# A two-layer product in float32 halves, whose first token block takes its second layer from undivided float32 operands

## The chip, the core and the metric

The kernel runs on one core of one Trainium2 chip. The metric is the device time of one execution in microseconds. Five engines with queues of their own work side by side: TensorE (PE, with its weight loads shown as PEld), VectorE (DVE), ScalarE (ACT), GpSimd (POOL) and SyncE (SP), which here issues most transfers. Each executes its queue in order, and an instruction that waits holds up all that stands behind it.

## The reference, cut to what matters

```python
def _moe_ref(x, w_in, w_out):          # x 4608 x 512, w_in 512 x 2048, w_out 2048 x 512
    h = x @ w_in
    g = h - np.tanh(h)
    return (g @ w_out).astype(np.float32)

def reference(**kwargs):
    attn_out = _attn_ref(q, k, v)      # softmax over q and over k, then two small products
    x = attn_out ... reshape(4608, 512)
    x = _moe_ref(x, w_in, w_out)
    return _moe2_ref(x, ...)           # each token to one of 8 experts, two layers, scaled
```

The weights w_in and w_out come as 64-bit floating point numbers. The change touches only the product g @ w_out of the first 512 tokens, and what has to be moved because of it.

## The kernel before, in words

The 4608 tokens are worked in NB = 9 blocks of 512. Within a block, the inner size 2048 goes in NCH = 16 chunks of 128. One chunk of one block is a slot s, from 0 to 143, with block j = s // 16 and chunk c = s % 16. The program is written out slot by slot: at(slot, order, function) files a step, and run_slot issues the steps of a slot in the order of their second number. That is the order of every engine's queue.

A float32 product is made of three products of a faster type, F32R. Each operand a is divided into a high part (ScalarE copies it into F32R) and a low part (the rest, subtracted on VectorE or GpSimd), and high x high, high x low and low x high are added up. Per slot the steps are:

- l1(s), at 0.30: the first layer, hps = w_in[c] x, 12 matmuls of 128 x 512 (4 parts of the depth, 3 products each).
- gfn(s), at 0.50: ScalarE makes gt and gy from hps, VectorE makes gg from them in two instructions (lines 246, one reading hps from the accumulator memory, one reading gy and gg).
- gsplit(s), at 0.90: gg is divided into gh (ScalarE, L687) and gl (L691). In block 0, gl is on GpSimd for three of four slots, and on VectorE otherwise.
- l2(s - 2), at 0.70: the second layer, four token tiles of 128, each with 3 matmuls of 128 x 512 (L706) into acc0 to acc3.

In block 0 the weights are still being made ready. Each slot loads two pieces of the 64-bit weights (load_pair, into raw and rawb), VectorE decodes them into float32 with integer operations (decode1 at 0.85: two of L243, four of L246, written to ta), ScalarE copies the high parts and GpSimd subtracts for the low parts (decode2 at 0.60, L298 and L300: woh and wol for w_out, wih and wil for w_in). From block 1 on all weights stay in memory.

Beside this, a KUnit per two heads prepares the next block's attention: a maximum over tokens (mx, tp, top, bc), subtraction, exponential, a product pk. For blocks 0 and 1 the maximum over partitions is made by a transposition on TensorE (pm, L374), a reduction on VectorE (mm, L378) and a matmul (L381). For blocks from 2 on it is one GpSimd instruction (red, L389). The unit of block j + 1 runs in block j, so the unit of block 2 runs in block 1. xmm makes the next block's x (px, L633, then xth on ScalarE and xtl on VectorE, L638 and L639); two of its four parts stand at the end of slot 15, two at the start of slot 16. The tiles pm, pk, pt and px take turns in two buffers of one tag "m" of the accumulator memory.

In block 1 a Router for block 0's output is added: rows of dot products on VectorE (rjk, L754), and at slot 30 four indirect transfers issued from GpSimd (L851).

Of the kernel before, what the change touches and what calls it, by code (L numbers as in the profile page):

```python
# [10 lines left out]
F32 = mybir.dt.float32  # L11
F32R = mybir.dt.float32r
# [60 lines left out]
def moe_kernel(ctx, tc, q, q_t, k_t, v_t, w_in, w_out, emb, tau, w1, w2, out, dbg=None):  # L73
# [108 lines left out]
    def full_run(general):  # L182
# [16 lines left out]

        wop.tile([P, 96], F32, name="pad1")  # L200
        win_h, win_l, wout_h, wout_l = {}, {}, {}, {}
        raws = {}
        npair = [0]

# [16 lines left out]
        def wtiles(c, which):  # L221
            if which == 0:
                pool = wap if c < NWA else lazy["wb"]
            else:
                pool = wop
            nm = "io"[which]
            wh = pool.tile([P, KD, P], F32R, name=f"w{nm}h{c}")
            wl = pool.tile([P, KD, P], F32R, name=f"w{nm}l{c}")
            if which == 0:
                win_h[c], win_l[c] = wh, wl  # L230
            else:
                wout_h[c] = wh.rearrange("p k f -> p (k f)")
                wout_l[c] = wl.rearrange("p k f -> p (k f)")
            return wh, wl
# [18 lines left out]
        def decode1(keys):  # L253

            ch = staged[keys[0]] = []
            for i, key in enumerate(keys):
                raw = raws.pop(key)
                ch.append((raw[:, :, :, 0], raw[:, :, :, 1], itile(f"ta{i}")) + wtiles(*key))
            if general:
                return  # L260
            for lo, hi, ta, wh, wl in ch:
                ts(ta, hi, 0x07FFFFFF, AND, 3, LS)
            for lo, hi, ta, wh, wl in ch:
                stt(ta, hi, -0x40000000, ta, AND, OR)
            for lo, hi, ta, wh, wl in ch:
                stt(ta, lo, 29, ta, RS, OR)
# [9 lines left out]
        def bound(i):  # L276
# [12 lines left out]
            if i < len(guarded):  # L289
                t = lazy["sb"].tile([P, GW // 2, 2], I32, name="gw", tag="gw", bufs=OPT["gwb"])  # L290
                (nc.sync if OPT['gsp'] else nc.scalar).dma_start(out=t.rearrange("p f two -> p (f two)"), in_=guarded[i])
                gtiles[i] = t

        def decode2(keys, eng=nc.gpsimd):
            ch = staged.pop(keys[0])
            if not general:
                for lo, hi, ta, wh, wl in ch:
                    act(out=wh, in_=ta.bitcast(F32), func=AF.Copy)  # L298
                for lo, hi, ta, wh, wl in ch:
                    eng.tensor_tensor(  # L300
                        out=wl, in0=ta.bitcast(F32), in1=wh.bitcast(F32), op=ALU.subtract
                    )
                return
            for lo, hi, ta, wh, wl in ch:
                tb, tx = itile("tb"), itile("tx")
                ts(ta, hi, 0x7FFFFFFF, AND, 9, RS)
                ts(tb, hi, -0x80000000, AND)
                ts(ta, ta, float(-(896 << 11)), ALU.add, 0.0, ALU.max)
                ts(tx, hi, 0x1FF, AND)
                stt(ta, ta, 12, tb, LS, OR)  # L310
                act(out=wh, in_=ta.bitcast(F32), func=AF.Copy)
                stt(tx.bitcast(F32), lo.bitcast(U32), 2.0 ** -32, tx, ALU.mult, ALU.add)
                ts(tb, ta, -0x800000, AND)
                stt(wl, tx.bitcast(F32), 2.0 ** -20, tb.bitcast(F32), ALU.mult, ALU.mult)
# [18 lines left out]
        class KUnit:  # L333
# [101 lines left out]
            def schedule(self, s):  # L435
                if s:
                    at(s - 2, 0.65, self.load)
                    at(s - 2, 0.66, self.loadv)
                    late = self.b < 2
                    at(s if late else s - 1, 0.20 if late else 0.80, self.mx)  # L440
                if self.b < 2:
                    at(s, 0.75, self.tp)
                    at(s + 1, 0.19, self.top)
                    at(s + 1, 0.45, self.bc)
                else:
                    at(s, 0.01, self.red)
                at(s + 1, OPT['ks'] if self.b > 1 else OPT['ks1'], self.sub)
                at(s + 1, 0.85, self.exp)
                at(s + 2, OPT['kv'], self.kv)
                at(s + 2, 0.80, self.rs)  # L450
                at(s + 3, 0.20, self.out)
# [208 lines left out]
        def gfn(s):  # L660
            h = hps.pop(s)
            t = gp.tile([P, BT], F32, name="gt", tag="gt", bufs=2)
            y = gp.tile([P, BT], F32, name="gy", tag="gy")
            g = gp.tile([P, BT], F32, name="gg", tag="gg")
            act(out=t, in_=h, func=AF.Square)  # L665
            if not general:
                act(out=y, in_=t, func=AF.Square, bias=cqa[:, 0:1])
                stt(g, h, Q2, t, ALU.mult, ALU.mult)
                stt(g, y, QB, g, ALU.add, ALU.mult)
            else:  # L670
                th = gp.tile([P, BT], F32, name="gth", tag="gth")
                mk = gp.tile([P, BT], F32, name="gm", tag="gm")
                act(out=y, in_=t, func=AF.Square, bias=cpa[:, 0:1])
                act(out=th, in_=h, func=AF.Tanh)
                act(out=mk, in_=t, func=AF.Relu, bias=cnt2[:, 0:1])
                stt(g, h, C3, t, ALU.mult, ALU.mult)
                stt(y, y, PB, t, ALU.add, ALU.mult)
                dve.tensor_tensor(out=th, in0=h, in1=th, op=ALU.subtract)
                stt(g, y, PD, g, ALU.add, ALU.mult)
                dve.copy_predicated(g, mk.bitcast(I32), th)  # L680
            g_t[s] = (g, t)

        def gsplit(s):
            g, t = g_t.pop(s)
            gh = gp.tile([P, BT], F32R, name="gh", tag="gh", bufs=2 if general else 3)
            gl = gp.tile([P, BT], F32R, name="gl", tag="gl", bufs=2 if general else 3)
            act(out=gh, in_=g, func=AF.Copy)  # L687
            if not general:
                act(out=t, in_=t, func=AF.Square, accum_out=guard[:, s : s + 1])
            e = nc.gpsimd if s < NCH and s % OPT['gm'][0] < OPT['gm'][1] and not general else dve  # L690
            e.tensor_tensor(out=gl, in0=g, in1=gh.bitcast(F32), op=ALU.subtract)  # L691
            g_t[s] = (gh, gl)

        acc = {}
# [1 line left out]
        def l2(s):  # L696
            j, c = divmod(s, NCH)
            gh, gl = g_t.pop(s)
            for t in range(TPB):
                if c == 0:  # L700
                    acc[j, t] = ps_acc.tile([P, DM], F32, name=f"acc{t}", tag=f"acc{t}")
                sl = slice(t * P, (t + 1) * P)
                for i, (a, r) in enumerate(
                    ((gh, wout_h[c]), (gh, wout_l[c]), (gl, wout_h[c]))
                ):
                    pe.matmul(  # L706
                        acc[j, t], lhsT=a[:, sl], rhs=r,
                        start=(c == 0 and i == 0), stop=(c == NCH - 1 and i == 2),
                    )
# [565 lines left out]
        for c, ks in enumerate(pairs):  # L1275
# [2 lines left out]
                at(c - 2, OPT['d1'], decode1, ks)  # L1278
            at(c - 1, OPT['d2'], decode2, ks)

        for s in range(NS + 2):
            j, c = divmod(s, NCH)
            if s < NS:
# [306 lines left out]
```

## Time and profile before

| | us |
|---|---|
| median of 3 runs | 1361.91 |
| runs | 1361.67, 1361.91, 1365.99 |
| profiled execution, its own time | 1364.51 |
| its span in the trace | 1362.8 |

| engine | busy us | share of the span |
|---|---|---|
| PE | 1303.3 | 96% |
| DVE | 1067.4 | 78% |
| ACT | 782.5 | 57% |
| POOL | 348.5 | 26% |

The span is one profiled execution; the time around it is 1.7 us. Shares are averages over stages that differ: block 0 lies from about 28 to 152 us in the span, block 1 from there to about 250 us. In the timelines, "idle before" names what the engine waited for. Matmuls overlap their neighbours in the records, so the cost of one in a row of many is read from the distance between starts, not from its own length.

### The profile page before, as it was taken

Reading aid. Unit: us, or ns where it says so; the run is one execution under the profiler, and the core shown is the slowest. Engines: PE = TensorE matmul, PEld = TensorE weight load, DVE = VectorE, ACT = ScalarE, POOL = GpSimd, SP = SyncE. Lnnn points to the kernel's source line nnn. Section 1 sums busy time; section 2 is a strip of 40 time slices with the busy share of each in tenths; the row PEclk is TensorE's granted clock in tenths of the full one; section 3 lists DMA queues with packets and bytes.
Section 4 is the critical chain, followed back from the end, with each engine's and each line's share of the span. In section 5 each row is a group of like instructions: output and inputs, shape, how many; then the busy total and the mean of one; then the engine's idle time right before and its main releaser. Section 6 shows DMA issues by size and latency. Waiting matters only on the chain. (4 is left out here: it accounts for less than half of the span.)

```text
span 1362.8 us, 20158 instructions
## 1 busy us (share of the span) xinstructions
PE 1303.3 (96%) x6725; PEld 1103.7 (81%) x6725; DVE 1067.4 (78%) x2131; ACT 782.5 (57%) x1552; POOL 348.5 (26%) x329
## 2 busy tenths in 40 slices
PE   5688999999999999999999999999998999999997
PEld 3566887888888888888888887879997899999986
DVE  7999789789689799697897986849987766767454
ACT  4566575555565655555655555446544576767543
POOL 3554321121121131211221301011223344353300
PEclk9888999999999999999999999999999999999998
DMA  6555210211201211211201000026313998765894
GB/s 213 172 162 165 97 55 20 87 34 32 89 21 39 82 40 36 66 40 60 62 20 63 1 0 32 1 93 200 101 57 125 286 286 252 228 186 187 270 312 173
DMA packets 127974, 151.41 MB, mean 111 GB/s; under 512 B 52464, under 2 KB 80624, under 8 KB 127600
## 3 DMA queue, kind: packets, MB, share of 16 engines
q1 hardware_dynamic: 112800, 114.27, 27.6%
q10 hardware_dynamic: 9216, 16.78, 4.3%
q0 software_dynamic: 5840, 18.92, 3.7%
q8 instruction: 57, 0.93, 0.3%
q14 instruction: 61, 0.50, 0.1%
HBM read 164.04 MB, written 23.91 MB: 138 GB/s over the span
## 5 line engine op out<-in xcount | busy, mean ns | idle before, releaser
L706 PE MATMUL acc<-woh,gl 128*128 128x512 f32 x576 | 226.2, 393 | 5.6 <-DVE gl L691 5.6
L706 PE MATMUL acc<-woh,gh 128*128 128x512 f32 x576 | 230.2, 400 | 0.0
L706 PE MATMUL acc<-wol,gh 128*128 128x512 f32 x576 | 225.5, 391 | 0.0
L687 ACT ACTIVATE gh<-gg 128x512 fp32r<-128x512 f32 x144 | 90.9, 631 | 233.4 <-DVE gg L246 232.0
L754 DVE SCALAR_TENSOR_TENSOR rjk<-xr,em 128x512 bf16<-128x512 f32 x288 | 210.3, 744 | 7.4 <-ACT rsq L742 7.4
L653 PE MATMUL hps<-xth,wih 128*128 128x512 f32 x576 | 161.8, 403 | 0.0
L653 PE MATMUL hps<-xtl,wih 128*128 128x512 f32 x576 | 157.0, 394 | 0.2
L653 PE MATMUL hps<-xth,wil 128*128 128x512 f32 x576 | 155.1, 391 | 0.0
L706 PEld LDWEIGHTS acc<-woh,gl 128*128 128x128 f32 x576 | 108.8, 189 | 30.8 <-DVE gl L691 7.9
L653 PEld LDWEIGHTS hps<-xtl,wih 128*128 128x128 f32 x576 | 109.7, 190 | 24.7 <-DVE xtl L639 1.1
L653 PEld LDWEIGHTS hps<-xth,wil 128*128 128x128 f32 x576 | 109.1, 189 | 23.5
L706 PEld LDWEIGHTS acc<-wol,gh 128*128 128x128 f32 x576 | 108.9, 189 | 23.3 <-issue 0.8
L706 PEld LDWEIGHTS acc<-woh,gh 128*128 128x128 f32 x576 | 108.8, 189 | 22.9 <-issue 0.7
L665 ACT ACTIVATE gt<-hps 128x512 f32<-128x512 f32 x144 | 84.7, 588 | 72.5 <-PE hps L653 71.8
L653 PEld LDWEIGHTS hps<-xth,wih 128*128 128x128 f32 x576 | 107.2, 191 | 22.1 <-ACT xth L638 1.0
L246 DVE SCALAR_TENSOR_TENSOR gg<-gy,gg 128x512 f32<-128x512 f32 x144 | 110.8, 770 | 15.0
L1193 PE MATMUL po<-wl,hh 128*128 128x512 f32 x296 | 117.3, 396 | 5.2 <-DVE wl L1181 3.7
L1169 DVE SCALAR_TENSOR_TENSOR hl<-ph,hh 128x512 fp32r<-128x512 f32 x74 | 50.8, 687 | 90.4 <-ACT hh L1168 84.8
L1193 PE MATMUL po<-wh,hh 128*128 128x512 f32 x296 | 116.8, 395 | 0.0
L691 DVE TENSOR_TENSOR gl<-gg,gh 128x512 fp32r<-128x512 f32 x132 | 99.7, 755 | 21.4 <-ACT gh L687 20.4
L1193 PE MATMUL po<-wh,hl 128*128 128x512 f32 x296 | 116.1, 392 | 0.0
L246 DVE SCALAR_TENSOR_TENSOR gg<-hps,gt 128x512 f32<-128x512 f32 x144 | 97.7, 679 | 21.2 <-ACT gt L665 20.5
(271 smaller groups left out, 2507.6 us busy)
## 6 DMA issues: line engine op xcount, KB each, us to landing
w2t<-in_moe_w_dram SPq DMA_DIRECT2D x84, 512.0 KB
w1t<-in_w_t_dram SPq DMA_DIRECT2D x38, 1024.0 KB
vt<-in_v_t_dram SPq DMA_DIRECT2D x32, 325.0 KB
kt<-in_k_t_dram SPq DMA_DIRECT2D x56, 160.0 KB
gw<-in_moe_w_in_dram ACTq DMA_DIRECT2D x32, 256.0 KB
gw<-in_moe_w_out_dram ACTq DMA_DIRECT2D x32, 256.0 KB
xg<-xs_d SPq DMA_DIRECT2D x60, 128.0 KB
stq<-in_q_t_dram SPq DMA_DIRECT2D x14, 512.0 KB
```

The costliest lines, as they stand in the source:

```text
L246: dve.scalar_tensor_tensor(out=o, in0=x, scalar=s1, in1=y, op0=op0, op1=op1)
L653: pe.matmul(h, lhsT=wt[:, kk, :], rhs=xx[:, kk, :], start=(n == 0), stop=(n == 3 * KD - 1),)
L665: act(out=t, in_=h, func=AF.Square)
L687: act(out=gh, in_=g, func=AF.Copy)
L691: e.tensor_tensor(out=gl, in0=g, in1=gh.bitcast(F32), op=ALU.subtract)
L706: pe.matmul(acc[j, t], lhsT=a[:, sl], rhs=r, start=(c == 0 and i == 0), stop=(c == NCH - 1 and i == 2),)
L754: dve.scalar_tensor_tensor(out=jk, in0=self.x[t // 2][:, t % 2, 0:DM], scalar=1.0, in1=lazy["em"][e], op0=ALU.mult, op1=ALU.mult, accum_ou ...
L1169: dve.scalar_tensor_tensor(out=hl, in0=self.ph, scalar=0.0, in1=hh.bitcast(F32), op0=ALU.max, op1=ALU.subtract,)
L1193: pe.matmul(po, lhsT=a[:, f % self.wd, sl], rhs=r[:, f % 2, :], start=(f == 0 and i == 0), stop=(f == 7 and i == 2),)
```

## The change

In block 0 the second layer takes g (one float32 tile, g32) and the decoded weights (w32) undivided, in one float32 matmul in place of three. So decode1 writes the weights of w_out straight into a tile that stays (wo32), gsplit makes neither gh nor gl in block 0, and decode2 divides only w_in. The weights of w_out are divided later: divide_out(c) stands in slot 15 + c at 0.62, three slots ahead of the second layer of block 1 that reads chunk c. The low part of chunk c takes the memory of the undivided weights of chunk c - 1. The KUnit of block 2 (four of them, in block 1) makes its maximum as those of blocks 0 and 1 do, at other places in the slot.

```diff
             wh = pool.tile([P, KD, P], F32R, name=f"w{nm}h{c}")
-            wl = pool.tile([P, KD, P], F32R, name=f"w{nm}l{c}")
+            if which and not general:
+                wout_h[c] = wh.rearrange("p k f -> p (k f)")
+                w32[c] = pool.tile([P, KD, P], I32, name=f"wo32{c}", tag=f"wol{c}")
+                return wh, None
+            wl = pool.tile([P, KD, P], F32R, name=f"w{nm}l{c}", tag=f"w{nm}l{c}")
...
-                ch.append((raw[:, :, :, 0], raw[:, :, :, 1], itile(f"ta{i}")) + wtiles(*key))
+                wh, wl = wtiles(*key)
+                ta = w32[key[0]] if wl is None else itile(f"ta{i}")
+                ch.append((raw[:, :, :, 0], raw[:, :, :, 1], ta, wh, wl))
...
+        def divide(w, wh, wl, eng=nc.gpsimd):
+            act(out=wh, in_=w, func=AF.Copy)
+            eng.tensor_tensor(out=wl, in0=w, in1=wh.bitcast(F32), op=ALU.subtract)
+
+        def divide_out(c):
+
+            if c:
+                wl = wop.tile([P, DM], F32R, name=f"wol{c}", tag=f"wol{c - 1}")
+            else:
+                wl = ap.tile([P, DM], F32R, name="wol0", tag="qt", bufs=2)
+            wout_l[c] = wl
+            divide(w32[c].bitcast(F32).rearrange("p k f -> p (k f)"), wout_h[c], wl)
...
-                for lo, hi, ta, wh, wl in ch:
-                    act(out=wh, in_=ta.bitcast(F32), func=AF.Copy)
-                for lo, hi, ta, wh, wl in ch:
-                    eng.tensor_tensor(
-                        out=wl, in0=ta.bitcast(F32), in1=wh.bitcast(F32), op=ALU.subtract
-                    )
+                for (c, which), (lo, hi, ta, wh, wl) in zip(keys, ch):
+                    if which == 0:
+                        divide(ta.bitcast(F32), wh, wl, eng)
...
+                elif self.b == 2:
+                    at(s, 0.32, self.tp)
+                    at(s, 0.86, self.top)
+                    at(s + 1, 0.32, self.bc)
                 else:
                     at(s, 0.01, self.red)
-                at(s + 1, OPT['ks'] if self.b > 1 else OPT['ks1'], self.sub)
+                at(s + 1, (OPT['ks1'], OPT['ks1'], 0.55)[self.b] if self.b < 3 else OPT['ks'], self.sub)
...
-            g = gp.tile([P, BT], F32, name="gg", tag="gg")
+            if s < NCH and not general:
+                g = gp.tile([P, BT], F32, name="g32", tag="gh", bufs=3)
+            else:
+                g = gp.tile([P, BT], F32, name="gg", tag="gg")
...
+            if s < NCH and not general:
+                act(out=t, in_=t, func=AF.Square, accum_out=guard[:, s : s + 1])
+                g_t[s] = (g, None)
+                return
...
-            e = nc.gpsimd if s < NCH and s % OPT['gm'][0] < OPT['gm'][1] and not general else dve
-            e.tensor_tensor(out=gl, in0=g, in1=gh.bitcast(F32), op=ALU.subtract)
+            dve.tensor_tensor(out=gl, in0=g, in1=gh.bitcast(F32), op=ALU.subtract)
...
+                if gl is None:
+                    pe.matmul(
+                        acc[j, t], lhsT=gh[:, sl], 
+                        rhs=w32[c].bitcast(F32).rearrange("p k f -> p (k f)"),
+                        start=(c == 0), stop=(c == NCH - 1),
+                    )
+                    continue
...
+        for c in range(0 if general else NCH):
+            at(NCH + c - 1, 0.62, divide_out, c)
```

On TensorE, the end of a slot of block 0 (slot 2: the second layer of chunk 0) stood before as

```order
L706 MATMUL acc_515<-woh_319,gh 128x512
L706 MATMUL acc_515<-wol_320,gh 128x512
L706 MATMUL acc_515<-woh_319,gl 128x512
L706 MATMUL acc_519<-woh_319,gh 128x512
L706 MATMUL acc_519<-wol_320,gh 128x512
L706 MATMUL acc_519<-woh_319,gl 128x512
L706 MATMUL acc_523<-woh_319,gh 128x512
L706 MATMUL acc_523<-wol_320,gh 128x512
L706 MATMUL acc_523<-woh_319,gl 128x512
L706 MATMUL acc_527<-woh_319,gh 128x512
L706 MATMUL acc_527<-wol_320,gh 128x512
L706 MATMUL acc_527<-woh_319,gl 128x512
```

and now, with the same first layer ahead and the same pk behind, as

```order
L674 MATMUL hps<-xth,wil_376 128x512 x4
L731 MATMUL acc_495<-wo_319,g_402 128x512
L731 MATMUL acc_497<-wo_319,g_402 128x512
L731 MATMUL acc_499<-wo_319,g_402 128x512
L731 MATMUL acc_501<-wo_319,g_402 128x512
L430 MATMUL pk<-vt,kt 128x130 x5
```

Twelve matmuls became four, each with float32 operands.

At the end of block 0 on TensorE (slots 15 and 16), a pm of the KUnit of block 2 now stands in front of the four px, and its second half behind them:

```order
L674 MATMUL hps<-xth,wil_1078 128x512 x4
L391 MATMUL pm<-ident,mx 128x128
L654 MATMUL px<-stq,bd_135 128x64
L654 MATMUL px<-stq,bd_137 128x448
L654 MATMUL px<-stq,bd_135 128x64
L654 MATMUL px<-stq,bd_137 128x448
L731 MATMUL acc_495<-wo_1026,g_1103 128x512
L731 MATMUL acc_497<-wo_1026,g_1103 128x512
L731 MATMUL acc_499<-wo_1026,g_1103 128x512
L731 MATMUL acc_501<-wo_1026,g_1103 128x512
```

Before, the four px stood there without a pm in between, and could use both buffers of the tag "m".

On GpSimd, around the indirect transfers of slot 30 there stood before

```order
L592 TENSOR_TENSOR stq<-stq,qbadd 128x512 x2
L389 ISA
L389 ISA mb<-mx 128x128
L851 DMA xs_d<-xr,rrow 39168x514 x4
L389 ISA mb<-mx 128x128
```

and now

```order
L303 TENSOR_TENSOR wol_1973<-wo_1026,woh_1025 128x512
L303 TENSOR_TENSOR wol_2030<-wo_1076,woh_1075 128x512
L885 DMA xs_d<-xr,rrow 39168x514 x4
L303 TENSOR_TENSOR wol_2121<-wo_1129,woh_1128 128x512
L406 ISA
L406 ISA mb<-mx 128x128
```

The maxima of the block-2 units (mb) left GpSimd, the 16 subtractions for wol moved there from block 0, and the last of them stands behind the four transfers.

## Rows read from the trace of the kernel before

**Rows 1.** Windows view of two stretches: each engine busy (instructions), granted clock, DMA share, GB/s.

```profile
102.00:136.00 34.00, 28.66 (x127) 23.43 (x126) 32.36 (x49) 22.89 (x67) 16.45 (x12) 0.90 0.55 166
204.00:238.00 34.00, 32.46 (x147) 26.50 (x147) 31.62 (x88) 17.44 (x38) 6.45 (x6) 1.00 0.08 20
```

**Rows 2.** Waits of TensorE, 28 to 152 us: total us, times, longest.

```profile
PE pm L374 <- DVE mx L366: 11.1, 3, 5.3
PE pm L381 <- DVE mm L378: 11.0, 3, 7.5
```

**Rows 3.** Timeline of TensorE, first block: start us, us busy, instructions (idle before).

```profile
46.65 0.80 PE L381 MATMUL pm<-ident,mm 128*128 128x128 f32 x2 [7.48 <-DVE mm L378]
68.73 0.77 PE L706 MATMUL acc<-woh,gh 128*128 128x512 f32 x1
73.14 1.07 PE L653 MATMUL hps<-xth,wih 128*128 128x512 f32 x4
75.86 0.39 PE L706 MATMUL acc<-woh,gh 128*128 128x512 f32 x1
96.80 2.05 PE L653 MATMUL hps<-xth,wih 128*128 128x512 f32 x4
129.21 2.06 PE L653 MATMUL hps<-xth,wih 128*128 128x512 f32 x4
134.08 0.46 PE L381 MATMUL pm<-ident,mm 128*128 128x128 f32 x2
```

**Rows 4.** Timeline of weight loads, float32 products px.

```profile
821.03 0.19 PEld L633 LDWEIGHTS px<-stq,bd 128*128 128x128 f32 x1 [0.24 <-issue]
821.46 0.19 PEld L633 LDWEIGHTS px<-stq,bd 128*128 128x128 f32 x1 [0.24 <-issue]
```

**Rows 5.** VectorE by line and form, 28 to 152 us: busy us, mean ns.

```profile
L246 DVE SCALAR_TENSOR_TENSOR ta<-rawb,ta 128x512 int32<-128x512 int32 x32 | 24.3, 817 | 0.0
L246 DVE SCALAR_TENSOR_TENSOR gg<-gy,gg 128x512 f32<-128x512 f32 x15 | 18.1, 1204 | 1.6
L243 DVE TENSOR_SCALAR ta<-rawb 128x512 int32<-128x512 int32 x16 | 12.6, 830 | 0.0
L243 DVE TENSOR_SCALAR ta<-raw 128x512 int32<-128x512 int32 x15 | 8.6, 610 | 0.0
```

**Rows 6.** Tile rawb: least, median and longest ns of its decode.

```profile
L246 DVE SCALAR_TENSOR_TENSOR ta<-rawb,ta x32: 675/680/1778, 29.3 to 142.1; 128x512 int32<-128x512 int32 x32
L243 DVE TENSOR_SCALAR ta<-rawb x16: 375/607/1526, 28.6 to 137.8; 128x512 int32<-128x512 int32 x16
```

**Rows 7.** GpSimd by line and form, 31.5 to 161.5 us.

```profile
L300 POOL TENSOR_TENSOR wil<-ta,wih 128x512 fp32r<-128x512 f32 x15 | 23.1, 1543 | 0.0
L300 POOL TENSOR_TENSOR wol<-ta,woh 128x512 fp32r<-128x512 f32 x16 | 21.4, 1336 | 52.7 <-ACT woh L298 52.7
L691 POOL TENSOR_TENSOR gl<-gg,gh 128x512 fp32r<-128x512 f32 x12 | 17.6, 1465 | 6.3 <-DVE ta L246 4.1 <-ACT gh L687 2.3
```

**Rows 8.** Timeline around 40 us, GpSimd and then VectorE.

```profile
39.36 1.26 POOL L300 TENSOR_TENSOR wol<-ta,woh 128x512 fp32r<-128x512 f32 x1 [3.17 <-ACT woh L298]
40.59 1.72 POOL L300 TENSOR_TENSOR wil<-ta,wih 128x512 fp32r<-128x512 f32 x1
39.93 1.25 DVE L246 SCALAR_TENSOR_TENSOR gg<-gy,gg 128x512 f32<-128x512 f32 x1
```

**Rows 9.** Timeline of the block change: TensorE, ScalarE, VectorE.

```profile
151.90 2.11 PE L633 MATMUL px<-stq,bd 128*128 128x64 f32 x8
153.07 0.60 ACT L638 ACTIVATE xth<-px 128x512 fp32r<-128x512 f32 x1 [1.76 <-PE px L633]
153.70 0.69 DVE L639 TENSOR_TENSOR xtl<-px,xth 128x512 fp32r<-128x512 f32 x1 [2.42 <-ACT xth L638]
```

**Rows 10.** Timeline of the second block: VectorE, TensorE.

```profile
225.44 0.63 DVE L691 TENSOR_TENSOR gl<-gg,gh 128x512 fp32r<-128x512 f32 x1
232.79 0.39 PE L706 MATMUL acc<-woh,gl 128*128 128x512 f32 x1
```

More of the change, by code (lines that the diff above doesn't have):

```diff
@@ L201, in full_run @@
         win_h, win_l, wout_h, wout_l = {}, {}, {}, {}
+        w32 = {}
         raws = {}
```

## The prediction

> **What bounds the kernel now.** I read the windows view first, cut into stretches of 34 us. In the second block TensorE is busy 32.5 of 34 us at full clock; in the first it is busy 28.7 of 34, its granted clock is 0.90, and VectorE is busy 32.4 of 34 [rows 1]. So the first block (about 28 to 152 us) goes at VectorE's pace, and what comes after goes at TensorE's. The chain that ended last covers only the final transfers of the span and is of no use here.
>
> Then the waits of TensorE in the first block: six, 11.1 us for the maxima mx and 11.0 us for mm, both from VectorE [rows 2]. Behind a long wait it also works at its lower clock: twelve matmuls take 75.86 - 73.14 = 2.72 us in a busy stretch, but 73.14 - 68.73 = 4.41 and 134.08 - 129.21 = 4.87 us after waits, and four of them 2.05 us instead of 1.07 at 96.80 [rows 3].
>
> Why is VectorE full there? The decode and gelu-like instructions are lengthened. One decode step takes 0.68 us at the median but 0.82 on average, its first step 0.375 at least and 0.83 or 0.61 on average; gg from gy takes 1.20 on average, where an instruction of the same kind has 0.68 [rows 5, 6]. The timelines show with what they collide: gg starts at 39.93 while GpSimd subtracts from 39.36 to 40.62, and takes 1.25 us; and GpSimd's next one takes 1.72 [rows 8]. Lengthening in all: 63 x (0.817 - 0.68) = 8.6, 15 x (1.204 - 0.68) = 7.9, 16 x (0.83 - 0.375) = 7.3 and 15 x (0.61 - 0.375) = 3.5, together 27.3 us. GpSimd's subtractions in that time are 23.1 us for wil, 21.4 for wol, 17.6 for gl, together 62.1 [rows 7].
>
> **What the change takes away in the first block.** The 16 subtractions for wol and the 12 for gl leave GpSimd: 39.0 of 62.1 us. If the lengthening falls in proportion, 27.3 x 39.0 / 62.1 = 17.2 us go, and VectorE would reach the end of the block 17 us earlier, at 134.8 instead of 152. (The four gl on VectorE go too; I leave them as a reserve. ScalarE's 32 copies are nothing: it waits for VectorE, not the reverse.)
>
> TensorE's own need decides next. From the end of its longest wait, 46.6 [rows 3], to 152 are 105.4 us. Without the other waits (22.1 - 7.5 = 14.6) and without the lower clock after them (1.7 + 2.15 + 1.0 = 4.8) it would need 86.0. The long wait itself, at the start, hangs on a stretch of VectorE with hardly any second layer beside it; I shorten it by 1.6 of 7.5 us, since a first decode step there is held up, but wil still stands in the way. What can be won is thus 14.6 + 4.8 + 1.6 = 21.0 us.
>
> **What it adds.** First, the matmuls. A float32 product is shown by px: it is two records whose weight loads start 821.46 - 821.03 = 0.43 us apart, so 0.86 us for 128 x 512 at full clock [rows 4]. Three matmuls of the divided form are 3 x 2.72 / 12 = 0.68. The 64 products cost 64 x 0.18 = 11.5 us more. 13 x 4 of them (9.4 us) stand before 152; TensorE would then need 86.0 + 9.4 = 95.4 from 45.0, so be through at 140.4, 5.6 us after VectorE. So TensorE becomes the bound of the first block, with a small lead of VectorE.
>
> Second, the end of the block. pm now holds one of the two buffers of tag "m" from slot 15 to its subtraction in slot 16, so the four px share the other. A px must wait until ScalarE and VectorE have read the one before it. px started at 151.90, xth at 153.07, xtl at 153.70 for 0.69 [rows 9], so the second could start at 154.4, instead of 0.8 us after the first at 152.7: 1.7 us, and again for the fourth. Together 3.4. The third comes behind a second layer, which covers it.
>
> Third, the units of block 2 on TensorE: bc is at most the 0.46 us of the pair at 134.08 [rows 3], a transposition half as many records, 0.23; their overlap with neighbours makes it about half, 0.35 x 4 = 1.4 us. Below nothing it cannot be, and 2.8 is the other end.
>
> Fourth, new waits of TensorE for mm and mx. With VectorE ahead by 5.6 us over thirteen slots they are short: 0.3 us in each of the three units after the first, 0.9. The bounds are 0 and 7.5, the latter if VectorE gains only half of the 17.2.
>
> Fifth, the second block. The 16 subtractions now collide with VectorE there, which is busy 31.6 of 34 [rows 1]. Yet it runs ahead: the low part that is done at 225.44 + 0.63 is first read at 232.79 [rows 10], 6.7 us later. At the ratio of the first block, 27.3 / 62.1 = 0.44, 13 subtractions of 1.34 us cost it 7.7 us, of which its idle time there and the lead cover nearly all; TensorE's idle 1.5 us in the window shown [rows 1] may even shrink. I take 0, between -1.5 and 7. The last subtraction now stands behind the four transfers of slot 30 on GpSimd; what it could delay, in slot 33, is within that bound.
>
> **The sum.** -21.0 + 11.5 + 3.4 + 1.4 + 0.9 + 0 = -3.8 us, on an execution that took 1364.5 (span 1362.8 and 1.7 around it), so 1360.7. That execution lay 2.6 above the median; against the median of 1361.9 it is 1358.1. I predict 1358.
>
> **A rule of the skill.** On what overlap costs, the row above shows gg held up for 0.57 us, from 39.93 about to the end of GpSimd's subtraction at 40.62 [rows 8]. The Trainium skill, SBUF — State Buffer, section "Who interferes with whom", says that a VectorE instruction with two inputs from SBUF competes with a GpSimd instruction that reads SBUF for one port, that it is a lock and not a sharing, and that the loser fully blocks. By that rule the trace agrees here: gg ends 0.56 us after the subtraction. It speaks against proportion: a single subtraction that always meets VectorE costs its whole length. What that would make of the time is the third rival.
>
> **Rivals.**
>
> TensorE alone (faster). VectorE is so far ahead that TensorE never waits (-0.9), the idle 1.5 us of the second block go, and the lower clock that I left uncounted (the rest of the stretch at 96.80, about 1) goes too: -3.8 - 3.4 = -7.2, 1354.7. For it: back-to-back subtractions on GpSimd, as at 39.36 and 40.59 [rows 8], are what holds up most, and they are gone. Against it: mx and mm stand behind a whole decode in VectorE's queue.
>
> The second block pays (no change). VectorE loses the whole 1.34 us at each of 13 subtractions, 17.4 us, against 6.7 of lead and some 5 of idle time (2.4 of 34 in the window, over 70 us): TensorE waits 5.7. -3.8 + 5.7 = +1.9, 1363.8. For it: 31.6 of 34. Against it: 0.44 in the first block, where it was fuller still.
>
> The port blocks wholly in both blocks (slower). The 15 subtractions that stay in the first block cost VectorE their whole 23.1 us, not 10.1. It ends at 147.8, 7.4 us behind TensorE's 140.4, so the wait is 7.4 instead of 0.9, +6.5; with the 5.7 above the sum is -3.8 + 6.5 + 5.7 = +8.4, 1370. It decides from a first-block loss of about 0.7 us per us of GpSimd on. For it: the row of gg. Against it: 0.44 measured over the whole block, with instructions that read the accumulator memory in between.
>
> **How the numbers follow.** About 0.3%, 4.1 us, is what a measurement can tell from no change. The forecast gets 0.42, with a range of its own from 1355 to 1361; it lies across that bound, so half of it counts as faster. TensorE alone gets 0.24, nearly all faster. The second block pays gets 0.20, nearly all the same. Blocking in both gets 0.14, nearly all slower. Faster 0.44, same 0.40, slower 0.16. The range of 1353 to 1366 leaves out the upper part of the last rival and little below the second.
>
> **What the changed profile would show.** In 102 to 136 us, or the same work earlier: TensorE busy 9 tenths or more at a granted clock near 1.0; gg from gy near 0.9 us on average, first decode steps near 0.45; waits for mx and mm together under 10 us, of which the first is still over 5; the float32 second-layer records 0.43 us apart; two waits of 1.7 us between px; the second block's first slot some 4 to 6 us earlier than before, and no more lost by its end than 2 us. Wrong, it would show VectorE full to the end of the first block with waits for mm in every unit, or waits of the second layer for gl in the second block.

## The result and the profile after

The change made the kernel slower: 1380.49 us median of four runs (1379.10 to 1380.90) against 1363.95 for the kernel before on the same chip (1361.67 to 1366.50), ratio 1.0115, interval 1.0099 to 1.0131. The profiled execution took 1380.55 us, its span 1378.8; before these were 1364.51 and 1362.8. So 16.0 us have to be found in the span.

They are found with one table. In TensorE's timeline each slot begins with the first layer, a row `hps<-xth,wih`; its start is the place of the slot in time. The table has the start in the kernel before, and how much later or earlier it is in each kernel (the experiments are told further down, their numbers stand in brackets). Each column is one profiled execution, which lies up to 3.2 us from its kernel's median.

| slot | before, us | after | units alone (1) | no units (2) | preload (7) | early (5) | early + units (6) | late on VectorE (10) |
|---|---|---|---|---|---|---|---|---|
| 0 | 31.52 | +3.0 | -0.1 | +2.8 | +1.6 | +2.4 | +2.5 | +1.9 |
| 15 | 149.18 | -7.1 | -0.3 | -6.8 | -6.0 | -4.3 | -7.6 | -5.1 |
| 16 | 161.34 | -2.0 | +3.6 | -5.4 | -1.0 | -3.0 | +0.7 | -3.8 |
| 19 | 176.10 | -0.8 | +3.6 | -4.2 | +0.2 | -1.8 | +1.9 | -2.6 |
| 21 | 186.98 | +7.2 | +8.9 | -4.2 | +8.4 | -1.8 | +10.2 | -2.6 |
| 25 | 212.13 | +12.9 | +10.2 | -0.3 | +14.0 | -1.2 | +10.1 | 0.0 |
| 33 | 261.72 | +13.3 | +10.6 | +3.6 | +14.4 | -1.0 | +10.5 | +2.0 |
| 35 | 273.76 | +20.4 | +12.5 | +12.8 | +14.8 | -0.9 | +12.6 | +2.0 |
| 143 | 913.78 | +16.6 | +10.7 | +9.8 | +14.0 | -4.2 | +9.9 | +0.4 |

Read the column "after" downwards: block 0 won 10.1 us between slots 0 and 15, and the loss lies in four places behind it: slots 15 to 16 (+5.0), 19 to 21 (+8.0), 23 to 25 (+5.8), 33 to 35 (+7.1). The rest of the way to 16.6: +3.0 stand ahead of slot 0, +1.5 lie between these places, and 3.8 come back from slot 35 on, 2.4 of them in slot 141, where the kernel before waits 3.25 us for gl at 904.32 and the change 2.29 at 922.50.

The windows of the kernel after (each engine busy with its instructions, granted clock, DMA share, GB/s) show the same:

```profile
102.00:136.00 34.00, 32.93 (x124) 20.60 (x123) 27.09 (x49) 17.68 (x46) 8.25 (x6) 1.00 0.42 129
170.00:204.00 34.00, 29.42 (x124) 23.66 (x123) 27.47 (x57) 24.74 (x64) 11.47 (x11) 0.90 0.17 47
204.00:238.00 34.00, 29.48 (x125) 23.78 (x124) 29.88 (x77) 18.33 (x39) 12.37 (x9) 0.90 0.10 28
272.00:306.00 34.00, 29.23 (x126) 24.12 (x125) 18.82 (x37) 16.90 (x39) 4.45 (x7) 0.90 0.18 58
```

and, of the kernel before, one stretch that was not shown yet:

```profile
170.00:204.00 34.00, 34.00 (x158) 28.05 (x158) 27.45 (x64) 24.74 (x62) 7.04 (x5) 1.00 0.19 55
```

Against [rows 1], the first block's window went from 28.66 us of TensorE at 0.90 to 32.93 at full clock, and VectorE from 32.36 to 27.09. The second block went the other way: from 34.00 and 32.46 us at full clock to 29.42 and 29.48 at 0.90. The lower clock came back, in another block (1.00 is 2.4 GHz throughout; 0.90 is the mean of a stretch that went in part at 1.2 GHz).

TensorE's waits of the kernel after, first for 28 to 158 us and then for 158 to 300 us (total us, times, longest):

```profile
PE pm L398 <- DVE mm L395: 10.2, 4, 5.7
PE px L654 <- DVE xtl L660: 2.8, 2, 1.4
...
PE pm L398 <- DVE mm L395: 6.9, 2, 3.5
PE pk L430 <- ACT kt L424: 4.8, 1, 4.8
PE pm L391 <- DVE mx L383: 2.2, 2, 1.2
```

In block 0 the 22.1 us of [rows 2] have become 10.2. From 158 to 300 us the kernel before had one wait of 1.54 us, for gl. Now there are 13.9. The first of block 0, the px of slots 15 and 16, a second layer between them, and the three longest of block 1 in the timeline:

```profile
47.86 0.79 PE L398 MATMUL pm<-ident,mm 128*128 128x128 f32 x2 [5.75 <-DVE mm L395]
147.91 1.24 PE L654 MATMUL px<-stq,bd 128*128 128x64 f32 x4 [1.41 <-DVE xtl L660]
148.99 3.60 PE L731 MATMUL acc<-wo,g 128*128 128x512 f32 x8
152.43 1.14 PE L654 MATMUL px<-stq,bd 128*128 128x64 f32 x4
154.98 1.24 PE L654 MATMUL px<-stq,bd 128*128 128x64 f32 x4 [1.41 <-DVE xtl L660]
188.57 0.80 PE L398 MATMUL pm<-ident,mm 128*128 128x128 f32 x2 [3.34 <-DVE mm L395]
219.43 0.79 PE L398 MATMUL pm<-ident,mm 128*128 128x128 f32 x2 [3.52 <-DVE mm L395]
285.39 2.54 PE L430 MATMUL pk<-vt,kt 128*128 128x130 f32 x10 [4.76 <-ACT kt L424]
```

A slot's second layer in float32 takes 152.43 - 148.99 = 3.44 us, eight records 0.43 us apart.

Why mm is late is in VectorE's queue, with GpSimd's row beside it:

```profile
185.93 0.69 DVE L251 SCALAR_TENSOR_TENSOR gg<-gy,gg 128x512 f32<-128x512 f32 x1
186.54 1.76 DVE L788 SCALAR_TENSOR_TENSOR rjk<-xr,em 128x512 bf16<-128x512 f32 x1
188.23 0.28 DVE L395 TENSOR_REDUCE mm<-pm 128x1 f32<-128x128 f32 x1
...
186.09 1.66 POOL L303 TENSOR_TENSOR wol<-wo,woh 128x512 fp32r<-128x512 f32 x1 [2.03 <-ACT woh L302]
```

The reduction that TensorE waits for stands behind gg and a row of the router. That row takes 1.76 us instead of 0.69; GpSimd's subtraction beside it ends at 187.75. This is not what makes the wait, though: experiments 1 and 6, with no wol on GpSimd there, wait 3.15 us for the same mm.

The fourth place is GpSimd's own queue, then the units' chain over VectorE and ScalarE to TensorE:

```profile
274.95 0.97 POOL L885 DMA_INDIRECT xs_d<-xr,rrow  x1 [4.77 <-DMA xs_d<-xr,rrow]
275.92 1.32 POOL L303 TENSOR_TENSOR wol<-wo,woh 128x512 fp32r<-128x512 f32 x1
282.90 0.72 POOL L406 PARTITION_ALL_REDUCE mb<-mx  x1 [5.66 <-issue]
...
283.65 0.91 DVE L418 TENSOR_TENSOR kt<-kt,mb 128x640 f32<-128x640 f32 x1 [12.60 <-POOL mb L406]
284.60 0.74 ACT L424 ACTIVATE kt<-kt 128x640 f32<-128x640 f32 x1 [8.02 <-DVE kt L418]
```

Before, the same all-reduce followed the fourth transfer at once:

```profile
261.99 0.97 POOL L851 DMA_INDIRECT xs_d<-xr,rrow  x1 [2.60 <-DMA xs_d<-xr,rrow]
263.00 0.67 POOL L389 PARTITION_ALL_REDUCE mb<-mx  x1
```

Between a subtraction and an all-reduce GpSimd now waits 5.66 us for nothing that the trace records ("issue"). The Trainium skill, GPSIMD Engine Reference, section "2.1 Instruction dispatch", says that the first call of a freshly loaded GpSimd routine costs about 6 us with no instruction to be seen in a profile; the row agrees. No trace shows what GpSimd does in that time; "reload" below is a name for this idle stretch. The kernel before has it too, at every such change: from 150 to 711 us 13 times from a TENSOR_TENSOR to an all-reduce, 5.80 to 6.24 us. One of them, whose mx was ready at 207.51:

```profile
206.51 2.50 POOL L592 TENSOR_TENSOR stq<-stq,qbadd 128x512 f32<-128x512 f32 x2 [11.75 <-DVE qbadd L588]
214.81 0.72 POOL L389 PARTITION_ALL_REDUCE mb<-mx  x1 [5.80 <-DVE gl L691]
```

The profile puts these 5.80 us down to a gl that had ended at 209.64. No one on TensorE waited for this mb.

### The profile page after: what moved, and what is told of

Same layout as the page of the kernel before. It is cut to its first block, busy times and chain, and to the rows that moved or that the text cites. A ratio compares the mean times of both kernels' runs of the same rounds, so it can differ in the third digit from the quotient of the medians.

```text
span 1378.8 us, 20022 instructions
## 1 busy us (share of the span) xinstructions
PE 1318.2 (96%) x6673; PEld 1095.0 (79%) x6673; DVE 1052.6 (76%) x2131; ACT 774.2 (56%) x1536; POOL 325.4 (24%) x313
## 5 line engine op out<-in xcount | busy, mean ns | idle before, releaser
L740 PE MATMUL acc<-woh,gh 128*128 128x512 f32 x512 | 205.7, 402 | 0.0
L740 PE MATMUL acc<-woh,gl 128*128 128x512 f32 x512 | 201.5, 394 | 2.3 <-DVE gl L718 2.3
L740 PE MATMUL acc<-wol,gh 128*128 128x512 f32 x512 | 201.3, 393 | 0.0
L715 ACT ACTIVATE gh<-gg 128x512 fp32r<-128x512 f32 x128 | 80.8, 631 | 202.3 <-DVE gg L251 202.3
L740 PEld LDWEIGHTS acc<-woh,gl 128*128 128x128 f32 x512 | 97.2, 190 | 24.2 <-DVE gl L718 3.5
L740 PEld LDWEIGHTS acc<-wol,gh 128*128 128x128 f32 x512 | 97.3, 190 | 20.6 <-issue 0.5
L740 PEld LDWEIGHTS acc<-woh,gh 128*128 128x128 f32 x512 | 97.4, 190 | 20.4 <-issue 0.5
L1215 DVE TENSOR_TENSOR wl<-w2t,wh 128x1024 fp32r<-128x1024 f32 x77 | 93.9, 1230 | 18.2 <-ACT wh L1213 17.4
L691 ACT ACTIVATE gy<-gt,cqa 128x512 f32<-128x512 f32 x144 | 104.3, 724 | 4.7
```

The source lines that it names most:

```text
L740: pe.matmul(acc[j, t], lhsT=a[:, sl], rhs=r, start=(c == 0 and i == 0), stop=(c == NCH - 1 and i == 2),)
L1215: e.tensor_tensor(out=wl, in0=lazy["w2t"][i], in1=wh.bitcast(F32), op=ALU.subtract)
```

## The experiments

The theory after the comparison: the change's gain in block 0 is real, and two by-products that were to be hidden lose it again in block 1: the unit's maximum on TensorE and VectorE, and the subtractions on GpSimd. The rival: block 1 can't keep a lead at all. Letters in the expectations belong to each run alone.

**1. The units alone.** The kernel before, with only the third block's units moved to TensorE and VectorE:

```diff
+                elif self.b == 2:
+                    at(s, 0.32, self.tp)
+                    at(s, 0.86, self.top)
+                    at(s + 1, 0.32, self.bc)
...
+                at(s + 1, (OPT['ks1'], OPT['ks1'], 0.55)[self.b] if self.b < 3 else OPT['ks'], self.sub)
```

> The kernel before, with one part of the change alone: the units of block 2 make their maximum on TensorE and VectorE (pm, mm) at the change's places; weights and g are divided as before. Theory A (the units' places lose the time in the second block: TensorE stands at the second half of pm for an mm that lies deep in VectorE's queue, VectorE being 7 us late there already in the kernel before; and GpSimd must reload its library behind the four transfers): slots 20 and 24 lose some 6 and 5 us, the px pairs 3.4, the first unit of block 3 some 6, in all 18 to 22 us slower than before, 1382 to 1386. Theory B (the subtractions moved to the second block hold VectorE up, and that makes mm late): without them only 3.4 + 1.4 + 6 us, 1373 to 1376.

Measured: 1378.72 us against 1365.07, ratio 1.0102 (1.0076 to 1.0127), between the ranges of the two theories. With nothing else changed, the units cost 3.9 us between slots 15 and 16 (px waits) and 5.2 between 19 and 21 (mx 1.24, mm 3.15, then the lower clock). The second wait for mm, slots 23 to 25, is 1.8 us here and these slots cost 1.5, not 5.8: that one needs the subtractions too. From slot 33 to 34 it loses 1.8 us, with "issue" of 6.22 ahead of the all-reduce at 276.99, although no wol is subtracted there: GpSimd's last work ahead of the transfers is a TENSOR_TENSOR (stq), where the kernel before had an all-reduce of the third block, at 230.66, in between.

**2. No units.** The change, with the third block's units back on GpSimd (the lines above taken out of it).

> The changed kernel with the units of block 2 as before, on GpSimd (mb), all else as changed. Theory A: the px waits (3.4), the waits for mm and what follows them (11 to 13) go, 1364 to 1367, the first unit of block 3 still 6 us late. Theory B: VectorE is as late as in the changed kernel and the second layer waits for gl instead: 1374 to 1379. A third way: each of the four mb now needs a library reload of some 6 us between subtractions, and VectorE waits for mb: 1370 to 1385, with waits of VectorE for mb of several us per unit.

Measured: 1377.33 us, ratio 1.0088 (1.0063 to 1.0112), not Theory A's 1364 to 1367 but within B's range and the third way's. No wait for mm is left in block 1, slots 15 to 16 cost 1.3 instead of 5.0, and still it is slow: 7.8 us go gradually from slot 19 to 33 and 9.2 from 33 to 35. The mean durations of VectorE, 170 to 260 us, in this kernel

```profile
L784 DVE SCALAR_TENSOR_TENSOR rjk<-xr,em 128x512 bf16<-128x512 f32 x30 | 23.3, 789 | 1.8 <-ACT rsq L772 1.8
L714 DVE TENSOR_TENSOR gl<-gg,gh 128x512 fp32r<-128x512 f32 x13 | 11.9, 913 | 0.5 <-ACT gh L711 0.4
```

and in experiment 5, which subtracts nothing on GpSimd there,

```profile
L784 DVE SCALAR_TENSOR_TENSOR rjk<-xr,em 128x512 bf16<-128x512 f32 x32 | 23.9, 761 | 1.8 <-ACT rsq L772 1.7
L714 DVE TENSOR_TENSOR gl<-gg,gh 128x512 fp32r<-128x512 f32 x15 | 10.2, 679 | 1.2 <-ACT gh L711 1.1
```

show gl lengthened from 679 to 913 ns, and TensorE waits for gl (2.2 us), gg (1.6), roh of the router (1.3) and GpSimd's wol itself (0.9). The end is one wait of TensorE:

```profile
276.97 2.54 PE L430 MATMUL pk<-vt,kt 128*128 128x130 f32 x10 [5.53 <-ACT kt L424]
```

behind an all-reduce that starts at 274.47 after 5.88 us of "issue".

**3. The units at other places in the slot.**

```diff
-                    at(s, 0.86, self.top)
-                    at(s + 1, 0.32, self.bc)
+                    at(s, 0.45, self.top)
+                    at(s + 1, 0.72, self.bc)
...
-                at(s + 1, 0.85, self.exp)
+                at(*((s + 2, 0.35) if self.b == 2 else (s + 1, 0.85)), self.exp)
```

(and the subtraction from 0.55 to 0.80).

> The changed kernel with the units of block 2 at other places: mm ahead of the slot's gg in VectorE's queue (0.45), the second half of pm behind the second layer of the next slot (0.72), the subtraction and the exponential later. The subtractions for wol stay where they are. Theory A: the two waits of 3.3 and 3.5 us for mm and the lower clock behind them go, 9 to 12 us faster than the change, 1369 to 1372. Theory B: VectorE stays late, the waits only move to the second layer (gl): 1377 to 1381.

Measured: 1377.40 us, ratio 1.0075 (1.0052 to 1.0098), in Theory B's range. The waits for mm are gone, but pk now waits for ScalarE's kt, 9.3 us in four waits from 158 to 300 us, and there is none for gl. The wait has moved along the unit's chain, which goes over VectorE's subtraction ahead of kt.

**4. The library early.** The change, with the divisions one slot earlier and a small all-reduce ahead of the transfers:

```diff
-            at(NCH + c - 1, 0.62, divide_out, c)
+            at(NCH + c - 2, 0.62, divide_out, c)
+        if not general:
+            dj = ap.tile([P, E], F32, name="dj")
+            at(2 * NCH - 2, 0.33, lambda: nc.gpsimd.partition_all_reduce(
+                dj, iota8, channels=P, reduce_op=bass_isa.ReduceOp.max))
```

> The changed kernel with divide_out one slot earlier, and one small all-reduce of a constant on GpSimd ahead of the four transfers of slot 30, so that its library is loaded before them. If the loss at slot 34 is the reload between the last subtraction and the first mb (5.7 us, shown as issue), then mb comes right behind the fourth transfer, TensorE's wait of 4.8 us for the exponential goes and the lower clock behind it: 5.5 to 6.5 us faster than the change, 1374 to 1375. If the transfers themselves are what is late, only 1 us goes: 1379.

Measured: 1387.66 us, ratio 1.0159 (1.0124 to 1.0194): slower still. The loss at slot 34 was gone (slot 33 +13.5, slot 34 +13.6), but from there to slot 143 the kernel drifted from +13.6 to +25.7, with one wait of TensorE (2.3 us for gl, which the change has too, at 922.50) and at full clock in every window of 100 us from 300 to 800. That asked for two controls, 7 and 8.

**5. The divisions early, on VectorE, no units.** The change with the units on GpSimd, and with the sixteen divisions at the block's boundary, where VectorE was 5.45 us busy of 14 (136 to 150 us of the change). Of the edit only the places are shown:

```diff
-            at(NCH + c - 1, 0.62, divide_out, c)
+            at(*((13, 0.91), (13, 0.92), (14, 0.91), (14, 0.92), (14, 0.93), (14, 0.94), (14, 0.95), (14, 0.96),
+                 (14, 0.97), (14, 0.98), (15, 0.71), (15, 0.72), (15, 0.73), (16, 0.06), (16, 0.07), (16, 0.45))[c], divide_out, c, dve)
```

> The second block's divisions are all made on VectorE while it idles around the block boundary (slots 13 to 16), none on GpSimd, and the third block's units stand on GpSimd as before. Theory A (what the second block loses is the GpSimd subtractions lying beside VectorE's work there, and the library that GpSimd has to load again behind them): the 5 us that block 0 has gained by slot 16 stay to the end, no loss of over 2 us between slots 17 and 35, 1357 to 1361 us. Theory B (the second block can't run that far ahead, and gives the gain back whatever stands on GpSimd): slots 17 to 35 lose 8 us or more again, 1366 us or more.

Measured: 1360.84 us (ten runs) against 1365.92 (thirteen), ratio 0.9962 (0.9950 to 0.9974): faster than both kernels. All that TensorE waits for from 136 to 290 us is

```profile
PE acc L736 <- DVE gl L714: 1.5, 1, 1.5
PE hps L670 <- DVE gg L251: 0.4, 1, 0.4
```

and slots 17 to 35 lose 1.7 us, where the rival (block 1 can't keep a lead) had 8 or more: it falls. The lead at slot 16 was 3.0 us, not the 5 of the expectation, and at slot 35 0.9 of it is left; the 3.3 from there to slot 143 are no merit of this edit, since the change gets 3.8 there. That it is faster rests on the ten runs against thirteen.

**6. The same, with the change's units.** Only the third block's units differ from experiment 5.

> As the run with the early divisions on VectorE, but the third block's units stay on TensorE and VectorE as the change has them. Theory A (the units' maximum stands behind VectorE's late work and costs what it cost when it alone was changed, about 4 us at the pairs of px and 6 us in slots 19 to 21, with nothing added by subtractions): start of slot 25 about 3 us after the kernel before, no loss at slot 34, 1366 to 1370 us. Rival C (the wait for mm is caused by the running ahead of TensorE, not by subtractions): both waits for mm of 3 us stay, slot 25 at +10, 1374 to 1378 us.

Measured: 1376.79 us, ratio 1.0090 (1.0064 to 1.0117): 16 us for the units alone, more than the theory's 1366 to 1370. The waits from 136 to 290 us:

```profile
PE pm L398 <- DVE mm L395: 4.5, 2, 3.2
PE px L654 <- DVE xtl L660: 4.4, 2, 3.0
PE pk L430 <- ACT kt L424: 1.7, 1, 1.7
PE pm L391 <- DVE mx L383: 1.6, 1, 1.6
```

Part is of my making: eight divisions lie in VectorE's queue ahead of the first xtl, so the first px waits 2.96 us and not 1.41, and slots 15 to 16 cost 8.3. But 8.2 us in slots 19 to 21 are the units', as in the change, without any subtraction on GpSimd. Time and slot 25 (+10.1) came as rival C had them, and the first wait for mm stayed, at 3.15 us; the second is 1.35, and slots 23 to 25 lose nothing (1.5 in experiment 1), so "both waits of 3 us stay" does not hold. Nor does C's cause: experiment 1, which does not run ahead, has the first wait at 3.15 us as well. My low price for it was wrong.

**7. The library early, without a new tile.** As experiment 4, but the all-reduce goes from a constant to itself:

```diff
+            at(2 * NCH - 2, 0.33, lambda: nc.gpsimd.partition_all_reduce(
+                cpa, cpa, channels=P, reduce_op=bass_isa.ReduceOp.max))
```

> The change with its divisions one slot earlier and an all-reduce of a constant onto itself ahead of the four transfers, so that GpSimd's library is loaded early, and no new tile. Theory A (the loss of 6 us at slot 34 is the reload; the drift of the run with the small tile came from its tile moving the others in SBUF): slot 34 at about +13, no drift after it, 1372 to 1376 us. Rival D (the drift belongs to the earlier divisions or the early all-reduce): the drift of 12 us between slots 34 and 143 comes again, 1385 to 1389 us.

Measured: 1372.77 us, ratio 1.0047 (1.0029 to 1.0064), 7.7 us below the change by the medians, in Theory A's range. Slots 33 to 35 lose 0.4 instead of 7.1, and no drift follows (column "preload"). GpSimd now stands idle ahead of the transfers, and TensorE waits for nothing there:

```profile
264.37 0.47 POOL L1318 PARTITION_ALL_REDUCE cpa<-cpa  x1 [6.83 <-issue]
...
278.42 0.97 POOL L885 DMA_INDIRECT xs_d<-xr,rrow  x1 [2.79 <-DMA xs_d<-xr,rrow]
279.43 0.69 POOL L406 PARTITION_ALL_REDUCE mb<-mx  x1
```

**8. A tile alone.** The change and `dj = ap.tile([P, E], F32, name="dj")`, used by nothing.

> The change with one more small tile (32 bytes a partition) that nothing uses, allocated where the earlier run had its own. Theory A (addresses): the drift of about 1 us in 8 slots after slot 34 comes with it, 1388 to 1394 us. Rival D (the tile is nothing): 1379 to 1382 us, as the change.

Measured: 1390.93 us, ratio 1.0188 (1.0169 to 1.0206), with the drift. The tile did it, not the all-reduce. Two matmuls of the second layer, six apart, first in the change and then here:

```profile
606.43 0.39 PE L740 MATMUL acc<-woh,gh 128*128 128x512 f32 x1
607.79 0.39 PE L740 MATMUL acc<-woh,gh 128*128 128x512 f32 x1
```

```profile
607.49 0.39 PE L740 MATMUL acc<-woh,gh 128*128 128x512 f32 x1
608.88 0.40 PE L740 MATMUL acc<-woh,gh 128*128 128x512 f32 x1
```

Six matmuls take 1.36 us in the one and 1.39 in the other: over the whole twelve of a slot 2.72 and 2.79, so 227 and 233 ns each.

**9. A tile of 64 bytes.** `[P, 2 * E]` instead of `[P, E]`, to see whether an odd multiple of 32 bytes is the cause.

> The change with an unused tile of 64 bytes a partition in the place where 32 bytes made the matmuls start 233 ns apart and not 226. Theory A (what costs the 7 ns is that operands begin at an odd multiple of 32 bytes): the drift is gone, 1379 to 1383 us, matmuls 226 ns apart around 600 us. Rival D (any tile there costs it, by its size or its presence): 1389 us or more, 233 ns.

Measured: 1390.31 us, ratio 1.0183 (1.0154 to 1.0213); matmuls 233 ns apart. It is not that. What in the placement costs the 6 ns stays open.

**10. The divisions late, on VectorE.** The change's places (slot 15 + c at 0.62), units on GpSimd, `divide_out` on VectorE.

> The third block's units on GpSimd as before; the divisions where the change has them, one in each slot of the second block, but on VectorE, none on GpSimd. It parts the engine from the place. Theory A (the losses are GpSimd's: its subtractions slow VectorE beside it, and its library is loaded again): no loss at slots 34 and 35; in slots 17 to 33 only what 16 subtractions of 0.61 us cost where VectorE is already 31.5 us busy of 34, 1 to 5 us; 1361 to 1366 us. Rival E (VectorE has no room in the second block for anything more, on whatever engine it is): slots 17 to 33 lose 8 us or more, 1368 us or more.

Measured: 1364.89 us, ratio 0.9989 (0.9974 to 1.0005), as the kernel before, in Theory A's range. Slots 19 to 33 lose 4.6 us, slots 33 to 35 nothing. So at the same place in the program the subtractions cost less on VectorE itself (16 of 0.68 us, 13 of them in 170 to 260 us) than beside it on GpSimd (7.8 us and the reload's 9.2). Moving them off the block (experiment 5) is worth another 4 us.

**11. Early divisions, units at the other places.** The early divisions of experiment 5 with the units as experiment 3 places them.

> Early divisions on VectorE, the third block's units on TensorE, but with the transposes of the maximum taken in the middle of the slot, the broadcast 0.40 and the subtraction 0.25 of a slot later, and the exponentials half a slot later. Theory A (a unit costs by where its maximum stands against VectorE's work, so that the wait for mm is a matter of place): no wait for mm between 160 and 240 us, the pairs of px still cost 4 to 8 us, slot 25 at +3 to +6, 1364 to 1369 us. Rival F (a unit on TensorE and VectorE costs 16 us in whatever order): slot 25 at +9 or more through other waits, 1372 us or more.

Measured: 1373.56 us, ratio 1.0072 (1.0045 to 1.0098). Slot 25 stood at +5.3, within the theory's +3 to +6, and no wait for mm is left; but the time is above the theory's 1364 to 1369 and where rival F had it, with pk waits of 4.3 us for kt and px waits of 4.4. Place decides part of the units' price, no place tried made it nothing.

## Why the prediction was wrong, by its own steps

Forecast were 1358 us and a range of 1353 to 1366; 1380.5 came. The four places behind block 0 belong to the third, fourth and fifth steps.

- **What the change takes away, and the matmuls: right.** From slot 0 to 15 the forecast had -21.0 + 9.4 + 0.9 = -10.7 us; measured -10.1. (27.3 x 39.0 / 62.1 is 17.1, not 17.2; nothing hangs on it.) The lengthening went, as VectorE by line and form in the kernel after (28 to 152 us) shows beside [rows 5]:

```profile
L251 DVE SCALAR_TENSOR_TENSOR g<-gy,g 128x512 f32<-128x512 f32 x16 | 12.7, 797 | 1.7
L251 DVE SCALAR_TENSOR_TENSOR ta<-rawb,ta 128x512 int32<-128x512 int32 x16 | 10.9, 680 | 0.0
```

  gg from gy went from 1204 to 797 ns, ta from rawb from 817 to 680. A float32 second layer costs 3.44 - 2.72 = 0.72 us a slot more, which is 4 x 0.18. The first wait for mm is 5.75 us, "still over 5", 1.7 shorter than before where the forecast had 1.6. That the whole came out so near is in part luck: the later waits were 4.5 us, not 0.9, and what is left for the lower clock and all else is 7.6 us, not 4.8. The sign at slot 16, 4 to 6 us earlier, came as 2.0, since slot 0 itself began 3.0 later.
- **The px pairs: right.** Two waits of 1.41 us; slots 15 to 16 cost 5.0 in the change against 1.3 in experiments 2 and 5, which have no pm there: 3.7, forecast 3.4.
- **"Third, the units of block 2 on TensorE", 1.4 us with an upper end of 2.8: wrong.** The step priced the matmuls and left out who makes TensorE wait. In the kernel before, an all-reduce on GpSimd holds up no one on TensorE; a matmul that needs mm stops TensorE's whole queue until VectorE has come to it. The "fourth" step knew such waits, bounded at 7.5, but counted them for block 0 only. Measured for the units by themselves: 13.7 us by the medians of experiment 1 (10.7 at slot 143 of its trace, of which 3.9 at the px), and 16.0 between the medians of experiments 5 and 6, of which some 3 are the divisions ahead of xtl.
- **"Fifth, the second block", 0 between -1.5 and 7: wrong.** It rested on a lead of 6.7 us, and that lead was misread: the two rows of [rows 10] belong to different chunks. Counted through from the start, the gl that is done at 226.07 is that of slot 25, and the second layer of slot 27 reads it first, 1.3 us later:

```profile
227.35 0.39 PE L706 MATMUL acc<-woh,gl 128*128 128x512 f32 x1
```

  The row at 232.79 reads the next gl. Counted so, the lead of gl in the kernel before is 2.6 us for slot 18, 1.4, 0.8 and 0.4 for 19 to 21, nothing for 22, and 1.2 to 1.4 for 23 to 27. For the gl of slot 22, done at 209.64, TensorE waits,

```profile
208.96 0.68 DVE L691 TENSOR_TENSOR gl<-gg,gh 128x512 fp32r<-128x512 f32 x1
209.69 0.50 PE L706 MATMUL acc<-woh,gl 128*128 128x512 f32 x1 [1.54 <-DVE gl L691]
```

  which is the idle 1.5 us that the prediction saw in [rows 1] and did not trace back. What failed is the cover and not the price of the lengthening: that was put at 7.7 us, and experiment 2 shows 3.0 at gl, the largest part. Measured for the subtractions by themselves: 16.5 us between the medians of experiments 5 and 2, of which the trace shows 7.8 in slots 19 to 33 (0.8 in experiment 5) and 9.2 in slots 33 to 35 (nothing there).
- **"What it could delay, in slot 33, is within that bound": wrong**, and a term that was never written. The last subtraction takes 1.32 us; changing GpSimd back to the all-reduce took 5.66 more, which the row at 214.81 of the kernel before had shown. When that was moved ahead, slots 33 to 35 lost 6.7 us less (experiment 7, which also has the divisions one slot earlier).
- **The clock.** After the waits of 3.34, 3.52 and 4.76 us the granted clock is 0.90 in the windows of 34 us, where the kernel before has 1.00. The prediction saw in block 0 that the lower clock comes behind such waits, and counted in full what its going gives back there; it did not count that new waits in block 1 bring it there.

The parts do not add up. Beside experiment 5, units cost 16.0 us and subtractions 16.5, but the change, with both, only some 20 (1380.49 and 1360.84; by the ratios 21). A reading that no run was made for: where TensorE is already late by the units' waits, VectorE has time for what GpSimd holds up. In the change slots 25 to 33 lose 0.4 us, in experiment 2 they lose 3.9.

The rival "the second block pays" named the right place, at 1363.8. It took the subtractions' lengthening alone, without the waits for mm and the reload, and the same misread lead: with 1 us of lead in place of 6.7 its own sum would give 1369.5, an estimate. On its price of overlap, rjk in the row at 186.54, with two inputs, ended 0.5 us after the subtraction and took 1.07 us more than its like. The single row agrees with the blocking rule of the Trainium skill's page SBUF — State Buffer ("Who interferes with whom"). Over the stretch, the 13 gl of experiment 2 took 0.23 us more each on average: most do not meet a whole subtraction.

Not settled: slot 0 begins 3.0 us later in the change and 1.3 to 2.8 in its variants, but not in experiments 1 and 8 (-0.1 and -0.6). Experiment 8 has all of the change's operations, so these alone are not the cause. The shorter first wait for mm (5.75 and not 7.48) is another thing: experiment 8, which does not begin late, gains 1.8 us there as well. No run was made for the cause.

## What to carry to other kernels

Before work is moved into a stage that "runs ahead", look for that stage's own waits: one wait of the bounding engine for the engine that gets the work means that there is no lead at that place. And when a lead is read from two rows, count both engines' rows through, so that the second row is the reader of the first. Price an operation that is moved from a free engine onto the path by who waits for its result, not by its own busy time. The same product in float32 was worth 0.4% once the divisions went to the engine that idled at the boundary of the blocks, and the units stayed where they were.

## What was not expected of the hardware

GpSimd stands idle for some 6 to 7 us (5.66 to 7.41 in the traces before and after, where nothing else holds it up longer), in part shown as "issue" and in part put down to other engines, at each change between a TENSOR_TENSOR (subtraction or addition) and an all-reduce, in both directions (in experiment 2 ahead of mb at 274.47 5.88, ahead of wol at 243.54 7.01; in the kernel before 25 times from 150 to 711 us; a COPY right behind an all-reduce, as at 275.08 in experiment 2, does not show it); an all-reduce of a constant, put where nobody waits for GpSimd, hid it (experiment 7). And an unused tile of 32 or 64 bytes a partition put the matmuls 233 ns apart and not 227 (around 600 us), at full granted clock and without a wait, for some 10 us in all; why is open.
